# Sparse attention with a mixture block: the top-32 mask made on VectorE by a compare-and-multiply instead of signs on ScalarE and products on GpSimd

## The chip, the cores and the metric

The kernel runs on one core of a Trainium2 chip. Its engines work side by side, each through its own instructions in order: PE (TensorE, matmuls), DVE (VectorE), ACT (ScalarE), POOL (GpSimd) and SP, which issues the DMAs. The metric is the device time of one execution in microseconds; less is better.

## The reference

```python
scores = scale * np.matmul(q, k.transpose(0, 1, 3, 2))          # (4, 8, 576, 576), scale = 1/8
kth = np.partition(scores, -top_k, axis=-1)[..., -top_k:-top_k + 1]   # top_k = 32
mask = scores >= kth
scores = np.where(mask, scores, -1000000000.0)
scores = scores - np.max(scores, axis=-1, keepdims=True)
attn = np.exp(scores)
attn = attn / (np.sum(attn, axis=-1, keepdims=True) + 1e-09)
out = np.matmul(attn, v)
```

Its result goes, for each of the four batches, through two dense blocks (called MoE in the kernel): a rotation of x by angles x @ w_theta, mixing over tokens and channels, a ReLU residual, then a gated block with a normalisation and an output product. All of it is in float32.

## The kernel before

**Tiles.** Four batches of four visits (two heads each), nine tiles of 128 rows of scores to a visit: 144 tiles, worked in 72 pairs (G = 2). For each pair, DVE finds the 32 largest scores of every row.

**Attention of a pair, by lines.** PE makes scores into PSUM (L429), ACT copies them to `x` (L433; three buffers). `topk` on DVE: a network of maxima and minima that halves the candidates (L448, L449, first 576 wide, then 288), MAX8 on the losers (L452), then four rounds of MAX8 (L458) and three of MATCH_REPLACE (L461) on 160 candidates. `mx[:, :, 0]` is then the row maximum, `mx[:, :, 31]` the 32nd. A flag (L465) tells whether the network may have dropped a candidate; a second, exact pass at the end runs only if one is set. ACT makes two of the three columns of `cf` (L469, L470: minus an eighth of the maximum; a rounding margin), DVE the third (L471: the negated threshold). `weigh`, for each tile of the pair: ACT takes the sign of score minus threshold into `sg` (L480), then the exponential in place in `x` (L481); POOL multiplies both into `sg` (L482). `transpose`: PE turns `sg` (L491) and ACT clips it with ReLU into `ptb` (L492), so that negative products become zero. `values`: PE multiplies with v and a column of ones (L502, L513, L516); ACT takes the result (L522, L526), DVE and POOL divide (L542 to L547).

**Around it.** In the first pairs DVE, ACT and POOL also turn the 64-bit weights to float32 pairs (L147 to L194). From the second batch on, the MoE work of the batch before is woven in: matmuls into `ps_m` (L552 to L554, three for each product, from high and low parts), with helpers on DVE, ACT and POOL that all record L568. The last batch's MoE work follows when attention is over.

**Order.** The loop writes pair after pair: `topk` of pair g, `weigh`, `transpose` and `values` of pair g - 1, `scores` of a later pair, and a quota of MoE work between them. A scheduler with priorities then sets each engine's order: an instruction goes where it is expected to be ready. On the chip each engine keeps that order.

Of the kernel before, what the change touches and what calls it, by code (L numbers as in the profile page):

```python
# [10 lines left out]
F32 = mybir.dt.float32  # L11
F32R = mybir.dt.float32r
I32 = mybir.dt.int32
AF = mybir.ActivationFunctionType
OP = mybir.AluOpType
# [1 line left out]
NEG = -3.0e38  # L17
MAGIC = 12582912.0
TURN = 6.283185
ULP = 1.25 * 2.0 ** -24  # L20
LN_EPS = 1e-6


# [1 line left out]
def sparse_attention_then_moe_kernel(  # L25
# [21 lines left out]
    B, H, D, S = qT.shape  # L47
# [4 lines left out]
    G = 2  # L52
# [15 lines left out]
    att = ctx.enter_context(tc.tile_pool(name="att", bufs=2))  # L68
# [6 lines left out]
    act, dve, pool, pe = nc.scalar, nc.vector, nc.gpsimd, nc.tensor  # L75

    def f32(ap):
        return ap.bitcast(F32)
# [237 lines left out]
    def run(exact):  # L316
# [93 lines left out]
            nc.sync.dma_start(extra[p, 0:D], v[b, 2 * j + 1, r])  # L410

        GATE = {}
        X, SG, MX, PT = {}, {}, {}, {}
        PER = NP * NT

        def scores(n):
# [17 lines left out]

        def topk(g):

            x = X[g]
            mx = att.tile([128, G, 32], F32, name="mx")
            mm = att.tile([128, G, S], F32, name="mm", bufs=1)
            if exact:  # L440
                src, mr = ([t[:, i] for i in range(G)] for t in (x, mm))
            else:


                z = att.tile([128, G, QUARTER + 16], F32, name="z", bufs=1)
                for t, lo, mid, hi, win in ((x, 0, HALF, S, mm), (mm, 0, QUARTER, HALF, z)):
                    a, b = t[:, :, lo:mid], t[:, :, mid:hi]
                    dve.tensor_tensor(win[:, :, 0:mid], a, b, op=OP.max)  # L448
                    dve.tensor_tensor(mm[:, :, mid:hi], a, b, op=OP.min)  # L449
                for k, losers in enumerate((slice(LOSERS, S), slice(QUARTER, LOSERS))):  # L450
                    for i in range(G):
                        dve.max(out=z[:, i, QUARTER + 8 * k:QUARTER + 8 * k + 8], in_=mm[:, i, losers])  # L452
                src = [z[:, i] for i in range(G)]
                mr = [mm[:, i, 0:QUARTER + 16] for i in range(G)]
            for r in range(4):
                top = [mx[:, i, 8 * r:8 * r + 8] for i in range(G)]
                for i in range(G):
                    last = dve.max(out=top[i], in_=src[i])  # L458
                if r < 3:
                    for i in range(G):  # L460
                        dve.match_replace(out=mr[i], in_to_replace=top[i], in_values=src[i], imm_value=NEG)  # L461
                    src = mr
            kth = mx[:, :, 31]
            if not exact:
                dve.tensor_tensor(flags[:, g], z[:, :, QUARTER + 7::8], mx[:, :, 31:32].to_broadcast([128, G, 2]),  # L465
                                  op=OP.is_gt)

            cf = att.tile([128, G, 3], F32, name="cf", bufs=3)
            act.activation(cf[:, :, 0], mx[:, :, 0], AF.Copy, scale=-0.125)  # L469
            act.activation(cf[:, :, 1], kth, AF.Abs, scale=ULP)  # L470
            dve.scalar_tensor_tensor(cf[:, :, 2], cf[:, :, 1], 1e-37, kth, op0=OP.max, op1=OP.subtract)  # L471
            MX[g] = cf
            GATE[g] = last.ins

        def weigh(n):
            x, cf = X[n // G][:, n % G], MX[n // G][:, n % G]
            if n % G == 0:
                SG[n // G] = att.tile([128, G, S], F32, name="sg", bufs=2)
            sg = SG[n // G][:, n % G]
            act.activation(sg, x, AF.Sign, bias=cf[:, 2:3])  # L480
            act.activation(x, x, AF.Exp, bias=cf[:, 0:1], scale=0.125)  # L481
            pool.tensor_tensor(sg, x, sg, op=OP.mult)  # L482

        def transpose(n):
            x = SG[n // G].rearrange("p i n -> p (i n)")
            pt = psum.tile([128, 5, 128], F32, name="ps_t")
            ptb = att.tile([128, 5, 128], F32, name="ptb", bufs=2)
            k = (5, 4)[n % G]
            for c in range(k):
                lo = (c + 5 * (n % G)) * 128  # L490
                pe.transpose(pt[:, c, :], x[:, lo:lo + 128], ident)  # L491
            act.activation(ptb[:, 0:k], pt[:, 0:k], AF.Relu)  # L492
            PT[n] = ptb

        def values(n):
# [84 lines left out]
        class Lag:  # L580
# [5 lines left out]
            def step(self, f=None):  # L586
                if self.q:
                    self.q.pop(0)()
                if f is not None:
                    self.q.append(f)  # L590
# [46 lines left out]
        class Front:  # L637
# [37 lines left out]
            def keep(self, pt, h, l, x, engine):  # L675
                n = x.shape[-1]
                uact.activation(h, pt, AF.Copy)
                udve.tensor_copy(x, pt[:, :, 0:n])
                for q in range(128 // n):
                    q = slice(q * n, (q + 1) * n)  # L680
                    engine.tensor_tensor(l[:, :, q], x, f32(h[:, :, q]), op=OP.subtract)
# [244 lines left out]
        N = len(tiles)  # L926
# [7 lines left out]
        def advance(quota):  # L934

            nonlocal work, credit
            credit += quota
            while work is not None and credit > 0:
                c = next(work, None)
                if c is None:  # L940
                    work = None
                    break
                credit -= max(c, 250)
            if work is None:
                credit = min(credit, 0.0)
# [16 lines left out]
        def at(f, n):  # L962
            if 0 <= n < N:
                late = tiles[n][2] == NP - 1
                with tc.high_priority(offset=AHEAD + (EDGE if late else 0)):
                    f(n)
# [29 lines left out]
            next(conv, None)  # L996
        for g in range(N // G + 2):
            with tc.high_priority(offset=AHEAD):
                if g < N // G:
                    topk(g)  # L1000
                    with tc.issue_after(GATE[g]):
                        if g:
                            next(conv, None)
                        if g == SPLIT:
                            for _ in conv:
                                pass
            n0 = G * g
            for i in range(G):
                step(n0 + i)
                at(weigh, n0 - G + i)  # L1010
            q = FIRST_QUOTA if n0 < PER else QUOTA
            for i in range(G):
                at(scores, n0 + G + 1 + i)
                advance(q)
                at(transpose, n0 - G + i)
                advance(q)
                if i == G - 1:
                    at(values, n0 - G + i)
# [4 lines left out]
        advance(1e12)  # L1023

    run(False)
    flagged = nc.values_load(count[0:1, 0:1], min_val=0, max_val=128)
    with tc.If(flagged > 0):
        run(True)
# [42 lines left out]
```

## Time and profile before

| | us |
|---|---|
| three timed runs | 1000.35, 992.66, 991.75 (median 992.66) |
| the profiled execution | 986.55 |
| its span, first to last instruction | 984.8 |
| busy: PE | 854.1 (87%) |
| busy: DVE | 837.5 (85%) |
| busy: ACT | 626.2 (64%) |
| busy: POOL | 546.2 (55%) |

How to read it: the busy shares are means over stretches with different limits, so the table of stretches below says more than they do. A PE instruction's end is modelled. A DVE instruction's time runs from its start to its end, so time in which it stands still counts as busy.

### The profile page before, as it was taken

The numbers are of one execution on the slowest core, as the hardware profiler recorded it, in microseconds if no ns is written. First come the engines' busy times: TensorE is split into PE (matmuls) and PEld (weight loads), VectorE is DVE, ScalarE is ACT, GpSimd is POOL, SyncE is SP. The second block draws the span as 40 slices with busy tenths as digits, with TensorE's granted clock in tenths as the row PEclk, the third lists the DMA queues.
The fourth block names the chain that finished last, engine by engine and source line by source line (L and its number), as shares of the span: only waits on it lengthen the run. The fifth ranks groups of instructions, "written<-read, shape, count | busy, mean of one in ns | idle before, by whom it ended". The sixth has DMA issues, their size and how long they took to land.

```text
span 984.8 us, 17792 instructions
## 1 busy us (share of the span) xinstructions
PE 854.1 (87%) x5802; PEld 785.8 (80%) x5802; DVE 837.5 (85%) x2710; ACT 626.2 (64%) x1298; POOL 546.2 (55%) x476
## 2 busy tenths in 40 slices
PE   3656677785898999898998999799899999999997
PEld 2555666664797988897898998698889998889987
DVE  6999999899999998899999998999999951463552
ACT  5666767678767567777867777577957764350121
POOL 1686776658685854758385656375655553420030
PEclk9865676687899999999999999899999999999999
DMA  7797774647638463544461844352742645341221
GB/s 218 222 333 224 238 220 150 171 139 203 219 105 241 164 167 140 157 150 100 147 162 32 276 152 144 126 161 71 229 138 68 258 155 181 156 181 52 103 86 53
DMA packets 79393, 159.76 MB, mean 162 GB/s; under 512 B 36143, under 2 KB 40239, under 8 KB 71866
## 3 DMA queue, kind: packets, MB, share of 16 engines
q1 hardware_dynamic: 79290, 158.53, 51.0%
q8 instruction: 48, 0.79, 0.3%
q14 instruction: 55, 0.45, 0.1%
HBM read 108.63 MB, written 23.32 MB: 134 GB/s over the span
## 4 chain that ended last, share of the span: by engine, by line
DVE 46%; PE 32%; ACT 7%; DMA 7%; issue 4%; POOL 3%; SPq 1%; DVEq 0%; ACTq 0%; POOLq 0%
DVE mm L449 8%; PE ps_m L552 7%; DVE mx L458 7%; PE ps_m L553 7%; PE ps_m L554 7%; DVE mm L461 7%; DVE z L452 5%; DVE mm L448 4%; PE ps_v L513 4%; PE ps_s L429 2%; PE ps_t L491 2%; DVE F L568 2%; DMA q<-hi 2%; DVE z L448 2%; DVE cf L471 2%
## 5 line engine op out<-in xcount | busy, mean ns | idle before, releaser
L482 POOL TENSOR_TENSOR sg<-x,sg 128x576 f32<-128x576 f32 x144 | 213.0, 1495 | 150.9 <-ACT x L481 90.9
L513 PE MATMUL ps_v<-vc,ptb 128*128 128x65 f32 (+1 forms) x1280 | 176.6, 277 | 15.1 <-ACT ptb L492 15.1
L513 PEld LDWEIGHTS ps_v<-vc,ptb 128*128 128x128 f32 (+1 forms) x1280 | 167.4, 201 | 24.4 <-ACT ptb L492 18.5
L491 PE MATMUL ps_t<-ident,sg 128*128 128x128 f32 x648 | 132.0, 305 | 42.2 <-POOL sg L482 33.5
L480 ACT ACTIVATE sg<-x,cf 128x576 f32<-128x576 f32 x144 | 103.8, 769 | 56.0 <-DVE cf L471 53.2
L491 PEld LDWEIGHTS ps_t<-ident,sg 128*128 128x128 f32 x648 | 93.7, 166 | 53.9 <-POOL sg L482 39.0
L458 DVE MAX8 mx<-mm 128x8 f32<-128x160 f32 x432 | 118.9, 313 | 0.0
L433 ACT ACTIVATE x<-ps_s 128x576 f32<-128x576 f32 x144 | 92.4, 642 | 32.0 <-POOL sg L482 16.8
L429 PE MATMUL ps_s<-k,q 128*128 128x288 f32 x256 | 91.2, 367 | 24.1 <-ACT x L433 15.0
L552 PE MATMUL ps_m<-w_t,zah 128*128 128x288 f32 (+2 forms) x272 | 98.7, 363 | 11.3 <-DVE F L568 6.7
L481 ACT ACTIVATE x<-x,cf 128x576 f32<-128x576 f32 x144 | 108.0, 767 | 0.1
L492 ACT ACTIVATE ptb<-ps_t 128x640 f32<-128x640 f32 (+1 forms) x144 | 92.4, 642 | 13.2 <-PE ps_t L491 12.3
L554 PE MATMUL ps_m<-w_t,zal 128*128 128x288 f32 (+2 forms) x272 | 96.6, 355 | 0.6 <-DVE zal L568 0.4
L553 PE MATMUL ps_m<-w_t,zah 128*128 128x288 f32 (+2 forms) x272 | 96.5, 355 | 0.0
L452 DVE MAX8 z<-mm 128x8 f32<-128x312 f32 (+1 forms) x288 | 89.5, 372 | 1.9
L552 PE MATMUL ps_m<-w_t,zbh 128*128 128x288 f32 x288 | 85.9, 301 | 3.2 <-DVE F L568 1.9
L461 DVE MATCH_REPLACE8 mm<-mx,mm 128x160 f32<-128x160 f32 x288 | 87.0, 309 | 0.0
L553 PE MATMUL ps_m<-w_t,zbh 128*128 128x288 f32 x288 | 85.4, 300 | 0.6 <-DMA w_t<-d_spl 0.6
L554 PE MATMUL ps_m<-w_t,zbl 128*128 128x288 f32 x288 | 84.3, 299 | 1.0 <-POOL zbl L568 1.0
L552 PE MATMUL ps_m<-ph,w_t 128*128 128x288 f32 x256 | 76.8, 301 | 8.1 <-DMA w_t<-d_chh 4.3
L429 PEld LDWEIGHTS ps_s<-k,q 128*128 128x128 f32 x256 | 55.8, 218 | 33.1 <-ACT x L433 24.6
L449 DVE TENSOR_TENSOR mm<-x 128x576 f32<-128x576 f32 x72 | 82.2, 1141 | 0.0
(175 smaller groups left out, 2391.4 us busy)
## 6 DMA issues: line engine op xcount, KB each, us to landing
k<-hi SPq DMA_DIRECT2D x60, 144.0 KB, 2.6
kl<-raw SPq DMA_DIRECT2D x60, 144.0 KB, 3.1
vc<-in_v_dram SPq DMA_DIRECT2D x48, 128.0 KB, 2.8
w_t<-d_trh SPq DMA_DIRECT2D x4, 1152.0 KB, 5.2
w_t<-d_trl SPq DMA_DIRECT2D x4, 1152.0 KB
out_dram<-t SPq DMA_DIRECT2D x32, 144.0 KB, 2.2
raw<-in_q_dram SPq DMA_DIRECT2D x15, 288.0 KB, 3.0
q<-hi SPq DMA_DIRECT2D x30, 144.0 KB, 2.8
```

The source lines that it names most:

```text
L429: pe.matmul(o, q, k[:, m], start=a == 0, stop=a == len(terms) - 1)
L449: dve.tensor_tensor(mm[:, :, mid:hi], a, b, op=OP.min)
L452: dve.max(out=z[:, i, QUARTER + 8 * k:QUARTER + 8 * k + 8], in_=mm[:, i, losers])
L458: last = dve.max(out=top[i], in_=src[i])
L461: dve.match_replace(out=mr[i], in_to_replace=top[i], in_values=src[i], imm_value=NEG)
L481: act.activation(x, x, AF.Exp, bias=cf[:, 0:1], scale=0.125)
L482: pool.tensor_tensor(sg, x, sg, op=OP.mult)
L491: pe.transpose(pt[:, c, :], x[:, lo:lo + 128], ident)
L513: pe.matmul(o, pt[:, c, q], chunks[:, c, slot], start=alone and c == 0, stop=not alone and i == 1 and c == 3)
L552: pe.matmul(out, ah, bh, start=first, stop=False)
L553: pe.matmul(out, ah, bl, start=False, stop=False)
L554: pe.matmul(out, al, bh, start=False, stop=last)
```

## The change

The exponentials no longer wait for the whole top-k. After the first round of MAX8, which gives the row maximum, ACT makes `most` (minus an eighth of it) and takes the exponentials from `x` into a tile of their own, `e`, which has the place and the two buffers of `sg`. When the 32nd largest is known, DVE does the rest in one instruction per tile (`keep`): where `x` >= 32nd, `e` stays, elsewhere it becomes 0. The signs (72 x 2), the margin (Abs), the threshold on DVE and the products on POOL are gone. `topk` becomes a generator with a stop after the exponentials, so that `keep` of pair g - 1 is written between the first round and the rest of pair g.

```diff
-X, SG, MX, PT = {}, {}, {}, {}
+X, E, MX, PT = {}, {}, {}, {}
@@ topk, in the loop over the rounds
                 for i in range(G):
                     last = dve.max(out=top[i], in_=src[i])
+                if r == 0:
+                    most = att.tile([128, G], F32, name="most", bufs=3)
+                    e = att.tile([128, G, S], F32, name="e", tag="sg", bufs=2)
+                    act.activation(most, mx[:, :, 0], AF.Copy, scale=-0.125)
+                    for i in range(G):
+                        act.activation(e[:, i], x[:, i], AF.Exp, bias=most[:, i:i + 1], scale=0.125)
+                    E[g], MX[g] = e, mx
+                    yield
@@ end of topk
-            cf = att.tile([128, G, 3], F32, name="cf", bufs=3)
-            act.activation(cf[:, :, 0], mx[:, :, 0], AF.Copy, scale=-0.125)
-            act.activation(cf[:, :, 1], kth, AF.Abs, scale=ULP)
-            dve.scalar_tensor_tensor(cf[:, :, 2], cf[:, :, 1], 1e-37, kth, op0=OP.max, op1=OP.subtract)
-            MX[g] = cf
             GATE[g] = last.ins
-        def weigh(n):
-            x, cf = X[n // G][:, n % G], MX[n // G][:, n % G]
...
-            act.activation(sg, x, AF.Sign, bias=cf[:, 2:3])
-            act.activation(x, x, AF.Exp, bias=cf[:, 0:1], scale=0.125)
-            pool.tensor_tensor(sg, x, sg, op=OP.mult)
+        def keep(g):
+
+            x, e, mx = X.pop(g), E[g], MX.pop(g)
+            for i in range(G):
+                dve.scalar_tensor_tensor(e[:, i], x[:, i], mx[:, i, 31:32], e[:, i], op0=OP.is_ge, op1=OP.mult)
@@ transpose
-            act.activation(ptb[:, 0:k], pt[:, 0:k], AF.Relu)
+            act.activation(ptb[:, 0:k], pt[:, 0:k], AF.Copy)
@@ main loop
+                steps = topk(g) if g < N // G else iter(())
+                next(steps, None)
+                if 0 < g <= N // G:
+                    keep(g - 1)
+                next(steps, None)
                 if g < N // G:
-                    topk(g)
...
-                at(weigh, n0 - G + i)
```

What the scheduler makes of it on DVE, at the border of two pairs in the middle of the program (pair 49 begins with L448 on `x`). Before:

```order
L458 MAX mx<-mm 128x8 x2
L465 TENSOR_TENSOR flags<-z,mx 128x4
L448 TENSOR_TENSOR mm<-x 128x2x288
L449 TENSOR_TENSOR mm<-x 128x2x288
L471 SCALAR_TENSOR_TENSOR cf<-cf,mx 128x2
L448 TENSOR_TENSOR z<-mm 128x2x144
L449 TENSOR_TENSOR mm<-mm 128x2x144
L452 MAX z<-mm 128x8 x4
```

After, at the same place (L472 is the flag, L480 the new instruction):

```order
L458 MAX mx<-mm 128x8 x2
L480 SCALAR_TENSOR_TENSOR e<-x,mx,e 128x576
L472 TENSOR_TENSOR flags<-z,mx 128x4
L448 TENSOR_TENSOR mm<-x 128x2x288
L449 TENSOR_TENSOR mm<-x 128x2x288
L480 SCALAR_TENSOR_TENSOR e<-x,mx,e 128x576
L566 TENSOR_SCALAR st<-st 128x1
L448 TENSOR_TENSOR z<-mm 128x2x144
```

The two L480 of the ended pair stand around the first two instructions of the next pair, ahead of its first round, and the tiny L471 is gone. (L566 is the MoE helper, L568 before.)

On PE, around the last transposes of the last pair. Before, in the middle of the product of the gate (`zah`):

```order
L554 MATMUL ps_m<-zah,w_t 128x288
L491 MATMUL ps_t<-ident,sg 128x128 x3
L513 MATMUL ps_v<-vc_103,ptb 128x65 x3
L491 MATMUL ps_t<-ident,sg 128x128
L513 MATMUL ps_v<-vc_103,ptb 128x65
L516 MATMUL ps_v<-vm_104,ptb 128x65
L552 MATMUL ps_m<-zah,w_t 128x288
```

After, in the next stage of the same batch, the mixing over tokens (`zbh`, `zbl`):

```order
L489 MATMUL ps_t<-ident,e 128x128
L511 MATMUL ps_v<-vc_103,ptb 128x65
L489 MATMUL ps_t<-ident,e 128x128
L511 MATMUL ps_v<-vc_103,ptb 128x65
L514 MATMUL ps_v<-vm_104,ptb 128x65
L552 MATMUL ps_m<-w_t,zbl 128x288 x3
L892 MATMUL ps_m<-w_t,zbh 128x288
```

The last transposes stand later in the MoE work: behind them come 1062 matmuls into `ps_m` before, and 931 after.

On ACT in after, one of the 36 pairs where other instructions stand between `most` (L462) and the exponentials (L464):

```order
L566 ACTIVATE zbl<-one 64x512 [waits PE_49]
L462 ACTIVATE most<-mx 128x2 [waits DVE_49]
L432 ACTIVATE x<-ps_s 128x576 [waits PE_49]
L566 ACTIVATE ph<-F 128x288 [waits DVE_49]
L464 ACTIVATE e<-x,most 128x576 [waits Activation_49]
L464 ACTIVATE e<-x,most 128x576
L490 ACTIVATE ptb<-ps_t 128x512 [waits PE_49]
```

A copy of scores that waits for PE (L432) and a MoE copy that waits for DVE stand ahead of the two exponentials there.

## Rows read from the trace of the kernel before

**Rows 1.** Table of stretches: us; busy PE, PEld, DVE, ACT, POOL; clock; DMA

```profile
0.00:301.00 301.00, 213.27 (x1162) 184.03 (x1163) 287.60 (x895) 207.99 (x412) 199.50 (x185) 0.77 0.67 204
301.00:797.00 496.00, 462.78 (x3436) 436.06 (x3435) 475.83 (x1619) 359.81 (x765) 301.43 (x245) 0.98 0.49 152
797.00:814.00 17.00, 17.00 (x122) 15.92 (x121) 4.59 (x24) 11.49 (x26) 7.39 (x9) 1.00 0.46 174
814.00:985.00 171.00, 161.02 (x1089) 149.75 (x1088) 69.44 (x175) 46.94 (x98) 37.85 (x40) 0.99 0.32 117
```

**Rows 2.** Instructions of a line: ns min/median/max, first and last start us, forms

```profile
L448 DVE TENSOR_TENSOR mm<-x x72: 696/752/3183, 12.0 to 787.1; 128x576 f32<-128x576 f32 x72
L448 DVE TENSOR_TENSOR z<-mm x72: 440/447/1687, 13.4 to 789.9; 128x288 f32<-128x288 f32 x72
L449 DVE TENSOR_TENSOR mm<-x x72: 743/754/6581, 12.7 to 787.9; 128x576 f32<-128x576 f32 x72
L449 DVE TENSOR_TENSOR mm<-mm x72: 402/457/1577, 13.9 to 790.4; 128x288 f32<-128x288 f32 x72
L465 DVE TENSOR_TENSOR flags<-z,mx x72: 147/164/2337, 20.6 to 796.8; 128x4 uint8<-128x4 f32 x72
L471 DVE SCALAR_TENSOR_TENSOR cf<-cf,mx x72: 100/156/1522, 20.7 to 797.7; 128x2 f32<-128x2 f32 x72
```

**Rows 3.** Groups by line: busy us, mean ns | idle before, and its releasers

```profile
L448 DVE TENSOR_TENSOR mm<-x 128x576 f32<-128x576 f32 x72 | 69.0, 958 | 11.4 <-ACT x L433 11.1
L448 DVE TENSOR_TENSOR z<-mm 128x288 f32<-128x288 f32 x72 | 35.7, 495 | 0.0
L449 DVE TENSOR_TENSOR mm<-x 128x576 f32<-128x576 f32 x72 | 82.2, 1141 | 0.0
L449 DVE TENSOR_TENSOR mm<-mm 128x288 f32<-128x288 f32 x72 | 41.2, 572 | 1.3
L465 DVE TENSOR_TENSOR flags<-z,mx 128x4 uint8<-128x4 f32 x72 | 29.1, 404 | 1.3
L471 DVE SCALAR_TENSOR_TENSOR cf<-cf,mx 128x2 f32<-128x2 f32 x72 | 28.9, 402 | 1.0 <-ACT cf L470 0.6
L482 POOL TENSOR_TENSOR sg<-x,sg 128x576 f32<-128x576 f32 x144 | 213.0, 1495 | 150.9 <-ACT x L481 90.9 <-issue 40.2 <-ACT cf L469 13.8
```

**Rows 4.** Timeline of DVE and POOL from 499 us: start, us, instruction

```profile
499.38 2.17 DVE L448 TENSOR_TENSOR mm<-x 128x576 f32<-128x576 f32 x1
501.47 2.10 DVE L449 TENSOR_TENSOR mm<-x 128x576 f32<-128x576 f32 x1
503.50 1.52 DVE L471 SCALAR_TENSOR_TENSOR cf<-cf,mx 128x2 f32<-128x2 f32 x1
...
499.38 5.62 POOL L568 TENSOR_TENSOR zbl<-xn,zbh 128x640 fp32r<-128x640 f32 x3
```

**Rows 5.** Timeline of DVE from 772 us, a pair with a free POOL

```profile
772.73 0.54 DVE L458 MAX8 mx<-z 128x8 f32<-128x160 f32 x2
...
776.79 0.77 DVE L465 TENSOR_TENSOR flags<-z,mx 128x4 uint8<-128x4 f32 x1
777.48 0.75 DVE L448 TENSOR_TENSOR mm<-x 128x576 f32<-128x576 f32 x1
778.15 0.74 DVE L449 TENSOR_TENSOR mm<-x 128x576 f32<-128x576 f32 x1
778.82 0.15 DVE L471 SCALAR_TENSOR_TENSOR cf<-cf,mx 128x2 f32<-128x2 f32 x1
```

**Rows 6.** Groups by line and shape: scalar_tensor_tensor on DVE

```profile
L148 DVE SCALAR_TENSOR_TENSOR w_f<-w_raw,w_f 128x512 int32<-128x512 int32 x16 | 12.0, 752 | 0.0
L568 DVE SCALAR_TENSOR_TENSOR st<-st 128x2 f32<-128x2 f32 (+1 forms) x64 | 14.8, 232 | 1.7
```

**Rows 7.** Timeline of PE: the last transpose, and matmuls of the tail

```profile
813.99 0.28 PE L491 MATMUL ps_t<-ident,sg 128*128 128x128 f32 x1
838.70 0.56 PE L554 MATMUL ps_m<-w_t,zbl 128*128 128x288 f32 x3
```

## The prediction: what bounds the kernel, the change part by part, and the numbers

> **What bounds the kernel now.** I read the table of stretches first [rows 1]. The profiled execution falls into three parts. Up to 301 us VectorE (DVE) is busy 287.60 us of 301 and TensorE (PE) only 213.27: DVE sets the pace alone. From 301 to 797 us DVE is busy 475.83 of 496 and PE 462.78: DVE still has the least room, 20 us, with PE close behind at 33. The last flags row starts at 796.8 us [rows 2], so the last top-k ends there. After it PE is full: it is busy all of the next 17 us and 161.02 of the last 171. The time is therefore the end of the last top-k (T, now 797) plus a tail that PE works off (now 984.8 - 797 = 188 us).
>
> In the first two parts DVE is busy 287.60 + 475.83 = 763.4 us of 797, and 33.6 us idle. So whatever DVE gets on top must show, beyond those 33.6 us. But not all of its busy time is work. The two large maxima and minima at L448 and L449 have medians of 752 and 754 ns [rows 2] and means of 958 and 1141 ns [rows 3]. The timeline shows the reason: at 499.38 us an L448 takes 2.17 us while three GpSimd subtractions run for 5.62 us, the L449 behind it takes 2.10, and a two-element L471 takes 1.52 [rows 4]. With a free GpSimd the same lines take 0.75, 0.74 and 0.15 us [rows 5]. I read it so: a DVE instruction with two SBUF inputs stands still while GpSimd (POOL) works on SBUF data. The lost time, 72 times mean less median in each of six rows, is 14.8 (L448, 576 wide), 27.9 (L449, 576 wide), 3.5 and 8.3 (the 288-wide ones), 17.3 (L465) and 17.7 us (L471) [rows 2, 3]: 89.5 us, of which 71.8 without L471.
>
> **The change part by part.** *Added on DVE:* 144 scalar_tensor_tensor of 128x576 (L480 of after), two SBUF inputs each. No row of before has just this one. The nearest are the max and min of the same width: with GpSimd free, one starts 0.67 us behind the other (777.48 to 778.15 to 778.82) [rows 5]. A scalar_tensor_tensor costs no more per element than these: 128x512 with two inputs has a mean of 752 ns, standing still included [rows 6]. 144 x 0.67 = **+96.5 us**.
>
> *Removed on DVE:* 72 L471, busy 28.9 us in all [rows 3]: **-28.9**.
>
> *Removed on POOL:* 144 products, 213.0 us busy [rows 3], of the POOL's 199.50 + 301.43 + 7.39 + 37.85 = 546.2 [rows 1], so 39%. If they caused the standing still in proportion, their end would give back 0.39 x 71.8 = 28 us; if they always lay beside the MAX8 instructions, which do not stand still (L458, 0.54 us for two in rows 5), nothing. The product follows the exponential, which follows cf, so it mostly falls into the next pair's MAX8: I take half, **-14**.
>
> *New standing still:* the 144 new instructions have two SBUF inputs too. The five remaining kinds lose 71.8 us in 360 instructions, 0.20 us each; 61% of that stays when the products are gone: 144 x 0.12 = **+18**. Bounds: none, and as often as L449 loses today, 144 x 0.387 = 56 us. The Trainium skill, page "SBUF — State Buffer", section "Who interferes with whom", says that such an instruction contends with a GpSimd instruction that reads SBUF and that the later one waits until the earlier has finished; the 2.17 us of rows 4 agree. By that rule, with POOL still busy about 288 us of 876 and half of 1.5 us (the mean of the products in rows 3) to wait for, the estimate would be 144 x 0.33 x 0.75 = 36 us in place of 18, and the end 18 us later.
>
> *Moved:* the scheduler puts more MoE work ahead of the last transposes: 1062 matmuls into ps_m stand behind them on PE before, 931 after. On DVE this brings 2 F instructions and 36 small st ones ahead of the last top-k; at 232 ns for an st one [rows 6] and 0.45 for F, **+9 us**. The tail gets shorter: the trace of before has 931 such matmuls left in the row at 838.70 us [rows 7], that is 146 us before the end. Between the last top-k and the last transposes stand in after only the two new instructions (counted above) and a few matmuls; with those and the last values I take 6 us. Tail: **152 us in place of 188**. PE has the room: from 301 us to its last transposes (813.99) [rows 7] it is busy 462.78 + 17.00 = 480 us; 131 matmuls at 171/1062 = 0.16 us add 21, so 501 in a stretch that grows to some 550 (91%, now 93%).
>
> *Removed on ACT:* 144 Sign and 72 Abs. ACT is busy 359.81 of 496 [rows 1], so this frees time that nothing waits for: 0. *Moved on ACT:* the exponentials start after the first MAX8 pair (773.27) and are needed after the last one (776.79, the flags row) [rows 5]: 3.5 us for one small copy (about 0.2) and two exponentials (about 0.67 apart, as the 128x576 rows): 1.6 us. 2 us to spare: 0. If that cover is gone, DVE itself waits, with all its queue behind it. x is given back after the new product on DVE rather than after POOL's, which is no later: 0.
>
> Sum on DVE: 96.5 - 28.9 - 14 + 18 + 9 = +80.6 us, 1.1 us per pair. With the idle time unchanged T = 797 + 80.6 = 878 and the span is 878 + 152 = 1030 us; with the 1.8 us around the span, 1032. The profiled execution itself took 986.55 us, 6 below the median 992.66 of the three runs and 5 below the lowest; such offsets are as likely to go either way in the next runs, so I forecast **1030 us**.
>
> **The rivals.** *A, a free port: faster.* Place: L448, L449, L465. If without the products POOL's other work fits into the MAX8 stretches, all 71.8 us come back and the new instructions lose nothing: 96.5 - 28.9 - 71.8 + 9 = +5, T = 802, end 954; PE would just allow it (its 854 us of busy time plus the 87.7 us that it is idle in the first 301 make 942). It decides when the sum on DVE falls under +28 (T + 152 under 977 to 980, over 1% below the median with the 1.8 us). For it: the lost time is there. Against: POOL keeps 333 us of other work, and rows 4 show a subtraction, not a product, as the blocker. A middle case, a sum of +28 to +48, gives **no change**, about 990.
>
> *B, the old idle time takes it.* If DVE's waits of 33.6 us shrink to 14, because scores, PSUM results and weights come relatively earlier, 20 us go: 1010, still slower.
>
> *C, DVE waits for the exponentials.* In 36 of 72 pairs ACT's order has other instructions between `most` and the second exponential, many waiting on PE. If these 36 lose 0.6 us each: +22, 1052. Against: PE is less full than now.
>
> *D, standing still as L449 today:* +56 in place of +18, and nothing given back: 1030 + 52 = 1082.
>
> **How the numbers follow.** The forecast, 1010 to 1050 with B within it, has 0.72; C 0.08 (1050 to 1060); D and worse 0.06 (above 1060); no change, with the stretch up to 1003, 0.09; A 0.05. A difference of 1% (10 us around 992.66) is about what a measurement of this kernel can tell from none. Slower: 0.72 + 0.08 + 0.06 = 0.86. The range leaves out A, most of the no-change case and D, together just under 0.2: 1000 to 1060.
>
> **What would show it.** Right: 144 L480 with a median near 750 ns and a mean of 0.85 to 0.95; the last top-k at about 878 us and DVE busy above 95% up to there; the tail from there near 152 us; L448 and L449 with means a little lower than now; PE busy about 91% in the middle. Wrong: means of L448 and L449 near their medians (A); DVE idle before L480 on ACT (C); last top-k before 850 us; or PE still full when DVE ends, so that the tail stays near 188 us (then the end is 36 us later).

## The result, and the profile after

The changed kernel takes 1005.68 us (median of 1003.28 to 1006.95) where the kernel before takes 992.78: a ratio of 1.0117, 95% interval 1.0068 to 1.0166. It is slower by 1.2%, where 1030 us, 3.8%, was forecast. The profiled execution took 1006.95 us, its span 1005.1. The trace of the kernel before is of an execution 6 us under that kernel's median, so the two traces differ by 20.3 us where the medians differ by 12.9.

The table of stretches of the changed kernel, columns as in rows 1 (us; busy PE, PEld, DVE, ACT, POOL; clock; DMA share; GB/s), cut first at the end of the last MAX8 of the last pair, then by parts:

```profile
0.00:849.68 849.68, 723.70 (x4815) 661.43 (x4815) 803.30 (x2621) 492.59 (x1000) 295.97 (x296) 0.88 0.55 170
849.68:1005.07 155.39, 143.26 (x987) 134.70 (x987) 73.46 (x162) 41.18 (x83) 36.17 (x37) 0.99 0.28 101
...
0.00:327.00 327.00, 227.92 (x1233) 197.37 (x1234) 300.64 (x920) 186.17 (x360) 132.04 (x147) 0.75 0.65 198
327.00:851.00 524.00, 496.95 (x3593) 465.23 (x3592) 503.98 (x1704) 307.33 (x643) 165.25 (x151) 0.96 0.48 151
```

The same cut of the kernel before, at its last MAX8:

```profile
0.00:796.81 796.81, 675.86 (x4595) 619.89 (x4596) 763.27 (x2511) 567.65 (x1174) 500.74 (x430) 0.90 0.56 172
796.81:984.75 187.94, 178.21 (x1209) 165.86 (x1208) 74.19 (x199) 58.58 (x124) 45.43 (x47) 0.99 0.33 122
```

The shape of the forecast is there: the last top-k ends 52.9 us later, and the tail is 32.5 us shorter (155.4 us; 152 was forecast). What differs is the first number, 52.9 us in place of 81. Of it, 40.0 us are DVE's busy time (763.3 to 803.3) and 12.8 its idle time (33.5 to 46.4).

DVE's groups by line in the changed kernel (busy us, mean ns | idle before, and who ended it), to be held against [rows 3]:

```profile
L480 DVE SCALAR_TENSOR_TENSOR e<-x,mx,e 128x576 f32<-128x576 f32 x144 | 139.7, 971 | 5.9 <-ACT e L464 5.7
L449 DVE TENSOR_TENSOR mm<-x 128x576 f32<-128x576 f32 x72 | 60.7, 843 | 0.0
L448 DVE TENSOR_TENSOR mm<-x 128x576 f32<-128x576 f32 x72 | 58.2, 808 | 2.2 <-ACT x L432 2.2
L449 DVE TENSOR_TENSOR mm<-mm 128x288 f32<-128x288 f32 x72 | 37.2, 517 | 0.9
L448 DVE TENSOR_TENSOR z<-mm 128x288 f32<-128x288 f32 x72 | 35.7, 496 | 0.1
L472 DVE TENSOR_TENSOR flags<-z,mx 128x4 uint8<-128x4 f32 x72 | 24.2, 336 | 0.0
```

A single L480 takes longer than forecast (971 ns on average, where 0.85 to 0.95 us was the sign of being right), but L449 fell from 1141 to 843 ns and L448 from 958 to 808 [rows 3], with a median of 751 ns for both (754 and 752 before): they stand still far less. The timeline of DVE at a place where POOL does not interfere, to be held against [rows 5] (start, us, instruction):

```profile
177.93 0.81 DVE L480 SCALAR_TENSOR_TENSOR e<-x,mx,e 128x576 f32<-128x576 f32 x1
178.66 0.75 DVE L448 TENSOR_TENSOR mm<-x 128x576 f32<-128x576 f32 x1
179.33 0.75 DVE L449 TENSOR_TENSOR mm<-x 128x576 f32<-128x576 f32 x1
180.00 0.81 DVE L480 SCALAR_TENSOR_TENSOR e<-x,mx,e 128x576 f32<-128x576 f32 x1
180.73 0.15 DVE L472 TENSOR_TENSOR flags<-z,mx 128x4 uint8<-128x4 f32 x1
```

A free L480 takes 0.73 us from its start to the next, an L448 0.67 as taken.

### The profile page after: what moved, and what is told of

Same layout as the page of the kernel before. It is cut to its first block, busy times and chain, and to the rows that moved or that the text cites. A ratio compares the mean times of both kernels' runs of the same rounds, so it can differ in the third digit from the quotient of the medians.

```text
span 1005.1 us, 17503 instructions
## 1 busy us (share of the span) xinstructions
PE 867.0 (86%) x5802; PEld 796.1 (79%) x5802; DVE 876.8 (87%) x2782; ACT 533.8 (53%) x1082; POOL 332.1 (33%) x332
## 4 chain that ended last, share of the span: by engine, by line
PE 42%; DVE 28%; DMA 12%; ACT 6%; POOL 5%; SPq 3%; issue 3%; ACTq 0%; POOLq 0%; DVEq 0%
PE ps_m L550 9%; PE ps_m L552 9%; PE ps_m L551 9%; DVE e L480 6%; PE ps_v L511 6%; PE ps_s L428 4%; DVE mm L469 4%; DVE mx L458 3%; PE ps_t L489 3%; DVE mm L449 3%; DMA k<-hi 2%; DMA q<-hi 2%; DVE mm L448 2%; DMA raw<-in_q_dram 2%; DVE z L452 2%
## 5 line engine op out<-in xcount | busy, mean ns | idle before, releaser
L489 PE MATMUL ps_t<-ident,e 128*128 128x128 f32 x648 | 142.8, 313 | 66.9 <-DVE e L480 59.1
L511 PE MATMUL ps_v<-vc,ptb 128*128 128x65 f32 (+1 forms) x1280 | 181.9, 279 | 18.0 <-ACT ptb L490 17.8
L511 PEld LDWEIGHTS ps_v<-vc,ptb 128*128 128x128 f32 (+1 forms) x1280 | 172.7, 203 | 28.6 <-ACT ptb L490 21.5
L432 ACT ACTIVATE x<-ps_s 128x576 f32<-128x576 f32 x144 | 92.9, 645 | 146.0 <-DVE e L480 103.8
L489 PEld LDWEIGHTS ps_t<-ident,e 128*128 128x128 f32 x648 | 97.7, 170 | 82.7 <-DVE e L480 39.6
L480 DVE SCALAR_TENSOR_TENSOR e<-x,mx,e 128x576 f32<-128x576 f32 x144 | 139.7, 971 | 5.9 <-ACT e L464 5.7
L550 PE MATMUL ps_m<-w_t,zah 128*128 128x288 f32 (+2 forms) x272 | 99.5, 366 | 6.8 <-DVE F L566 4.7
L464 ACT ACTIVATE e<-x,most 128x576 f32<-128x576 f32 x144 | 103.8, 769 | 1.2
L551 PE MATMUL ps_m<-w_t,zah 128*128 128x288 f32 (+2 forms) x272 | 97.9, 360 | 0.0
L452 DVE MAX8 z<-mm 128x8 f32<-128x312 f32 (+1 forms) x288 | 90.0, 372 | 1.9
L566 POOL TENSOR_TENSOR pl<-F,ph 128x288 fp32r<-128x288 f32 x52 | 47.6, 923 | 116.7 <-ACT ph L566 97.0
L428 PE MATMUL ps_s<-kl,q 128*128 128x288 f32 x256 | 81.4, 329 | 1.3 <-DMA kl<-raw 1.3
L373 POOL TENSOR_TENSOR raw<-raw,hi 128x576 fp32r<-128x576 f32 x30 | 46.8, 1559 | 107.5 <-ACT hi L372 91.0
```

The costliest lines, as they stand in the source:

```text
L428: pe.matmul(o, q, k[:, m], start=a == 0, stop=a == len(terms) - 1)
L432: act.activation(x.rearrange("p (c n) -> p c n", c=2), ps[:, :, 0:HALF], AF.Copy)
L464: act.activation(e[:, i], x[:, i], AF.Exp, bias=most[:, i:i + 1], scale=0.125)
L480: dve.scalar_tensor_tensor(e[:, i], x[:, i], mx[:, i, 31:32], e[:, i], op0=OP.is_ge, op1=OP.mult)
L511: pe.matmul(o, pt[:, c, q], chunks[:, c, slot], start=alone and c == 0, stop=not alone and i == 1 and c == 3)
L550: pe.matmul(out, ah, bh, start=first, stop=False)
```

## The experiments

Ten kernels were run. Four were to tell whether the price of the removed products, or the place of the new instruction, was mis-sized; the later ones where that price comes from. This table holds the time, the ratio to the kernel before with its interval, the busy time of DVE and POOL over the whole span, and the end T of the last MAX8. Each ratio is taken to executions of the kernel before that were timed beside that kernel (their medians lie between 991.3 and 995.0 us), so it compares two rows better than their times do. DVE, POOL and T are those of one profiled execution.

| kernel | us | ratio (95%) | DVE | POOL | T |
|---|---|---|---|---|---|
| before | 992.8 | | 837.5 | 546.2 | 796.8 |
| after | 1005.7 | 1.0117 (1.0068 to 1.0166) | 876.8 | 332.1 | 849.7 |
| e1 before, no products | 957.1 | 0.9592 (0.9556 to 0.9628) | 776.9 | 324.0 | 755.8 |
| e2 after, products added | 1106.9 | 1.1110 (1.1069 to 1.1150) | 999.1 | 560.3 | 949.2 |
| e3 after, no masking | 961.7 | 0.9643 (0.9609 to 0.9677) | 773.0 | 324.9 | 738.3 |
| e4 after, half masking | 978.6 | 0.9800 (0.9753 to 0.9847) | 834.3 | 334.9 | 812.5 |
| e5 e1 with memsets | 952.3 | 0.9595 (0.9539 to 0.9650) | 789.3 | 487.1 | 766.0 |
| e6 before, L471 to ACT | 1006.8 | 1.0144 (1.0087 to 1.0201) | 839.5 | 555.4 | 821.6 |
| e7 after, second tile's masking on POOL | 1041.3 | 1.0494 (1.0439 to 1.0549) | 892.2 | 619.5 | 859.1 |
| e8 before, products held back | 989.0 | 0.9959 (0.9937 to 0.9980) | 828.1 | 550.3 | 800.2 |
| e9 e8 with L471 to ACT | 1001.6 | 1.0092 (1.0060 to 1.0124) | 837.6 | 546.5 | 799.9 |
| e10 e2, products held back | 1032.3 | 1.0405 (1.0350 to 1.0460) | 912.4 | 506.6 | 877.8 |

### e1: the kernel before without the products

```diff
-            act.activation(x, x, AF.Exp, bias=cf[:, 0:1], scale=0.125)
-            pool.tensor_tensor(sg, x, sg, op=OP.mult)
+            act.activation(sg, x, AF.Exp, bias=cf[:, 0:1], scale=0.125)
```

> The kernel before without GpSimd's 144 products: the exponential overwrites the sign in sg, so the mask is left out of the result. Theory P (the products hold the port that DVE's two-input instructions need, directly and by keeping GpSimd's other work queued up): the means of L448 and L449 at 576 wide fall to about 0.8 and 0.85 us as in the changed kernel, DVE loses 60 us or more of busy time in all, the last top-k ends at 735 to 755 us, and TensorE becomes the limit, time 935 to 960. Theory Q (the products hardly matter, the time given back in the changed kernel came from where the new instruction stands): means of L448 and L449 stay above 0.95 and 1.1 us, DVE loses 30 us or less, last top-k at 770 to 795, time 965 to 985.

DVE's busy time fell by 60.6 us, as theory P said, and T by 41 to 755.8. (L449 stayed at 914 ns, above the 0.85 us of theory P.) Its groups by line:

```profile
L449 DVE TENSOR_TENSOR mm<-x 128x576 f32<-128x576 f32 x72 | 65.8, 914 | 0.0
L448 DVE TENSOR_TENSOR mm<-x 128x576 f32<-128x576 f32 x72 | 58.5, 812 | 13.2 <-ACT x L433 12.8
L449 DVE TENSOR_TENSOR mm<-mm 128x288 f32<-128x288 f32 x72 | 35.6, 495 | 0.6
L471 DVE SCALAR_TENSOR_TENSOR cf<-cf,mx 128x2 f32<-128x2 f32 x72 | 24.7, 342 | 5.8 <-ACT cf L470 5.5
L465 DVE TENSOR_TENSOR flags<-z,mx 128x4 uint8<-128x4 f32 x72 | 21.9, 304 | 1.3
```

Nothing was done to these instructions, yet L449 went from 1141 to 914 ns and L448 from 958 to 812. The 576-wide pair, the narrow L449 and L465 gave back 39.6 us (72 times the differences of the means), L471 another 4.3; the remaining 17 us lie in other DVE instructions, weight conversion and MoE helpers. T moved by less than the busy time, since DVE then idles 56.1 us of 755.8 instead of 33.5.

### e3: the changed kernel without the masking

```diff
-            for i in range(G):
-                dve.scalar_tensor_tensor(e[:, i], x[:, i], mx[:, i, 31:32], e[:, i], op0=OP.is_ge, op1=OP.mult)
```

> The changed kernel without the 144 masking instructions on DVE (the mask is left out of the result). If DVE sets the end of the top-k: their 129 us of DVE time go, of which some 20 come back as standing still of L448, so the last top-k ends at 735 to 755 us; 1236 MoE matmuls stand behind the last transposes, so the tail is 195 to 210 us and the time 935 to 960, with TensorE now the limit. If the masking lies largely beside waits that DVE has anyway, the last top-k ends after 790 us and the time is above 975.

T came to 738.3 and the tail to 223 us, because 1236 MoE matmuls were left behind it; the time, 961.7, lies 1.7 us above what was expected. DVE lost 103.8 us, not the 139.7 that L480 was busy:

```profile
L449 DVE TENSOR_TENSOR mm<-x 128x576 f32<-128x576 f32 x72 | 68.9, 956 | 0.0
L448 DVE TENSOR_TENSOR mm<-x 128x576 f32<-128x576 f32 x72 | 63.5, 882 | 3.0 <-ACT x L432 2.2
```

L448 and L449 are slower again, 882 and 956 ns in place of 808 and 843. The first L480 of a pair stands ahead of them in the queue, so this fits waits that L480 takes on itself and that otherwise fall on them.

e1 and e3 cut the change into three steps in DVE's busy time, which add up because each starts where the one before ends: products away 837.5 to 776.9 (-60.6); signs and L471 away and the exponentials moved ahead 776.9 to 773.0 (-3.9); masking added 773.0 to 876.8 (+103.8). Sum: +39.3, as measured.

### e4: half of the masking

```diff
-                dve.scalar_tensor_tensor(e[:, i], x[:, i], mx[:, i, 31:32], e[:, i], op0=OP.is_ge, op1=OP.mult)
+                dve.scalar_tensor_tensor(e[:, i, 0:HALF], x[:, i, 0:HALF], mx[:, i, 31:32], e[:, i, 0:HALF],
+                                         op0=OP.is_ge, op1=OP.mult)
```

> The changed kernel with the masking on only the first 288 of 576 columns (the other half is left unmasked). If DVE sets the end of the top-k and an element costs the same throughout: 144 x 0.30 = 43 us less on DVE, last top-k at 805 to 815 us, 995 matmuls behind the last transposes, time 965 to 980. If standing still rather than elements makes the new instruction's cost: less than 25 us, time above 980.

DVE lost 42.5 us and T 37, the time 27, since the tail grew to 172 us. The loss is that of L480 itself, from 139.7 us in the changed kernel:

```profile
L480 DVE SCALAR_TENSOR_TENSOR e<-x,mx,e 128x288 f32<-128x288 f32 x144 | 97.1, 675 | 8.1 <-ACT e L464 6.4 <-PE ps_s L428 1.7
```

So the elements of L480 are paid for on the path at 0.30 us per 288, as forecast from L448.

### e2: products put back into the changed kernel

```diff
+                pool.tensor_tensor(x[:, i], e[:, i], e[:, i], op=OP.mult)
```

> The changed kernel with 144 GpSimd products of 128x576 put back (exponential times itself, written over the used-up scores, which nobody reads). Theory P: GpSimd is as full as before the change, DVE's standing still comes back with 45 to 60 us, the last masking ends at 895 to 910 us and the time is 1045 to 1065. Theory Q: DVE gets at most 20 us more, time 1005 to 1025.

The products add work on used-up data, which nobody reads. The direction was right and the size far off: DVE gained 122 us, 0.85 us per product, and the time is 1106.9, above even the 1065 of theory P. As many products of that size cost DVE 0.42 us each in the kernel before (60.6 / 144), though each takes longer there when nothing holds it up (median 1.43 us, against 1.15 in e10, where a product reads one tile twice). The groups by line show who ends POOL's wait:

```profile
L481 POOL TENSOR_TENSOR x<-e 128x576 f32<-128x576 f32 x144 | 227.4, 1581 | 208.8 <-DVE e L480 155.3 <-DVE flags L472 21.3 <-DVE st L567 18.8
L449 DVE TENSOR_TENSOR mm<-x 128x576 f32<-128x576 f32 x72 | 99.7, 1385 | 0.0
L449 DVE TENSOR_TENSOR mm<-mm 128x288 f32<-128x288 f32 x72 | 63.8, 886 | 1.0
L448 DVE TENSOR_TENSOR z<-mm 128x288 f32<-128x288 f32 x72 | 60.9, 846 | 0.1
```

Here a product is released by L480 itself, and so starts just where L449 and the two 288-wide instructions follow: 138 of the 144 products lie beside a DVE instruction with two SBUF inputs, and 35 do in the kernel before (counted over the rows of both engines, with more than 0.05 us side by side). That raised the question whether the place of a product sets its price, or its number.

### e10: the same products, held back

```diff
@@ topk, behind the MAX8 on the losers
+                Z[g] = z
@@ keep, behind the masking
+            z = Z.get(g + 1, x)
+            after = pool.tensor_scalar(turn, z[:, 0, QUARTER:QUARTER + 1], 1.0, 0.0, op0=OP.mult, op1=OP.add)
+            with tc.issue_after(after.ins):
+                for i in range(G):
+                    pool.tensor_tensor(x[:, i], e[:, i], e[:, i], op=OP.mult)
```

> The changed kernel with the 144 GpSimd products of e2 (on used-up data, read by nobody), but held back until the next pair's first MAX8 on the losers is done, by a tiny GpSimd instruction that reads its result. The number and size of the products are those of e2; only their start differs. If the price of a product is set by where it starts: DVE's busy time, 877 without products and 999 in e2, comes to 890 to 930, last masking at 865 to 905, time 1020 to 1060. If each product costs 0.85 us wherever it stands: DVE 990 or more, time 1095 to 1115. If the products then push the other GpSimd work into the two-input stretch as much as they leave it: DVE 930 to 990, time 1060 to 1095.

(The lines that make `turn` and `Z` are left out here.) In the trace 933 MoE matmuls lie behind the last transposes, as in that of the changed kernel. The products are those of e2; their start differs, and a tiny instruction (L485) is added that holds them back. DVE's busy time is 912.4: 35.6 us over the changed kernel, 0.25 us per product in place of 0.85, and the time 1032.3 in place of 1106.9.

```profile
L488 POOL TENSOR_TENSOR x<-e 128x576 f32<-128x576 f32 x144 | 163.9, 1158 | 0.7 <-DVE e L483 0.7
L451 DVE TENSOR_TENSOR mm<-x 128x576 f32<-128x576 f32 x72 | 66.2, 919 | 0.0
L451 DVE TENSOR_TENSOR mm<-mm 128x288 f32<-128x288 f32 x72 | 40.1, 557 | 1.1
L485 POOL TENSOR_SCALAR turn<-z 128x1 f32<-128x1 f32 x71 | 13.6, 192 | 137.8 <-DVE z L454 137.4
```

The narrow L451 (L449 of the changed kernel) is back from 886 to 557 ns. Both engines gain: the products, now beside MAX8, take 1158 ns instead of 1581; 22 of 144 still meet a two-input instruction. Between e2 and e10, then, the price of one and the same product is set by where it starts. That MAX8 does not stand still beside a product can be read in the trace of the kernel before: 317 of its MAX8 on 160 columns lie beside one and take 313 ns on average, 97 lie beside no POOL instruction and take 312.

### e5: GpSimd held without reading

```diff
-            pool.tensor_tensor(sg, x, sg, op=OP.mult)
+            pool.memset(x, 0.0)
+            pool.memset(x, 0.0)
```

(and the exponential into `sg`, as in e1; the mask is left out of the result.)

> As the kernel before without products (e1), but with two GpSimd memsets of 128x576 over the used-up scores where each product stood: GpSimd's queue is held about as long, without reading anything. Theory D (each GpSimd instruction that reads holds DVE up by itself): DVE's busy time stays as in e1, 772 to 785 us, and the means of L448 and L449 at 576 wide near 0.81 and 0.83 us. Theory K (what costs is the full queue, which pushes GpSimd's other work into DVE's two-input stretch): if the memsets fill GpSimd by 150 us or more, DVE's busy time rises to 795 to 810. In both the time stays below 985.

The memsets keep POOL busy:

```profile
L482 POOL MEMSET x<- 128x576 f32 x144 | 83.0, 580 | 148.2 <-ACT sg L481 147.8
L483 POOL MEMSET x<- 128x576 f32 x144 | 82.9, 581 | 4.3
L449 DVE TENSOR_TENSOR mm<-x 128x576 f32<-128x576 f32 x72 | 70.3, 976 | 0.0
L448 DVE TENSOR_TENSOR mm<-x 128x576 f32<-128x576 f32 x72 | 62.4, 866 | 12.0 <-ACT x L433 11.3
```

166 us of them, in place of 213 of products, raise DVE's busy time from 776.9 to 789.3, a fifth of what the products cost. The measurement lies between the two expectations (D up to 785, K from 795), about as near the one as the other. The memsets themselves hold no max or min up: eleven 576-wide L448 and L449 ran beside nothing but memsets on POOL, and took 748 to 759 ns, as free ones do. The Trainium skill, page "SBUF — State Buffer", section "Who interferes with whom", states that a DVE instruction with two SBUF inputs contends with a GpSimd instruction that reads SBUF and not with one that only writes it; these eleven agree. So what these two lines lost against e1 (8.4 us) came with the fuller queue, which moves POOL's other work.

This does not show that the rest of the 60.6 us is the products' own reading. In the kernel before, the products lie only 13 us beside the wide L448 and L449, which gave back 26.9 us in e1. Over all DVE instructions, the time beyond each one's free time comes to some 129 us in the kernel before and 70 in e1, nearly all of it beside some POOL instruction; at most 35 us lie beside a product (estimates from the rows of both engines; in e2 up to 119 do). The other 25 or so of the 60.6 must have come through POOL's other work, which runs at other times without the products. Why the memsets cost less by that way is not shown; they held POOL for a shorter time.

### e6 and e9: the threshold made by ScalarE

```diff
-            dve.scalar_tensor_tensor(cf[:, :, 2], cf[:, :, 1], 1e-37, kth, op0=OP.max, op1=OP.subtract)
+            for i in range(G):
+                act.activation(cf[:, i, 2:3], kth[:, i:i + 1], AF.Identity, bias=cf[:, i, 1:2], scale=-1.0)
```

> The kernel before with the threshold column made by two tiny ScalarE instructions per pair instead of the tiny DVE instruction L471 (28.9 us busy, 17.7 of it standing still). If DVE sets the end and the standing still goes with the instruction: DVE busy 837 to 812, last top-k near 772, time 970 to 980. If the standing still only passes to the next two-input instruction: DVE busy 822 to 828, last top-k near 785, time 980 to 990.

> As e8, and the threshold column made by ScalarE instead of L471 (as in e6). If in e6 it was the products' earlier start into DVE's two-input stretch that took the gain away: with them held back DVE loses 15 to 29 us more than e8, time 945 to 970. If it was ScalarE's longer chain: time no better than e8, or worse.

Neither gained anything. In e6 DVE's busy time is 839.5 with L471 gone, where 812 to 828 was expected, and it idles 56.8 us before T (16.0 of them for the copies of scores on ACT, now fuller); the time is 1006.8. With the products held back (e9), DVE has 837.6 us against 828.1 in e8. Its groups, and under them those of e8:

```profile
L450 DVE TENSOR_TENSOR mm<-x 128x576 f32<-128x576 f32 x72 | 80.9, 1124 | 15.5 <-ACT x L434 15.0
L451 DVE TENSOR_TENSOR mm<-x 128x576 f32<-128x576 f32 x72 | 79.5, 1104 | 0.0
```

```profile
L450 DVE TENSOR_TENSOR mm<-x 128x576 f32<-128x576 f32 x72 | 71.1, 988 | 13.2 <-ACT x L434 12.6
L451 DVE TENSOR_TENSOR mm<-x 128x576 f32<-128x576 f32 x72 | 73.3, 1018 | 0.0
L474 DVE SCALAR_TENSOR_TENSOR cf<-cf,mx 128x2 f32<-128x2 f32 x72 | 20.0, 278 | 1.3 <-ACT cf L473 1.1
```

The 20.0 us of the tiny instruction (L474 here) are gone, and L450 and L451 at 576 wide alone stand 9.8 and 6.2 us longer. This fits a wait that falls on whatever stands first in the two-input stretch: remove that, and its neighbour takes it. But it is not all: DVE's other instructions gained 29.5 us in e9, more than the 20.0 that left. The products also lay worse, beside two-input instructions for 50 us in e9 against 36 in e8 (and 79 in e6 against 46 in the kernel before). These two runs do not separate the two causes.

### e7: one tile of each pair masked on GpSimd

```diff
-            for i in range(G):
-                dve.scalar_tensor_tensor(e[:, i], x[:, i], mx[:, i, 31:32], e[:, i], op0=OP.is_ge, op1=OP.mult)
+            dve.scalar_tensor_tensor(e[:, 0], x[:, 0], mx[:, 0, 31:32], e[:, 0], op0=OP.is_ge, op1=OP.mult)
+            pool.tensor_scalar(x[:, 1], x[:, 1], mx[:, 1, 31:32], None, op0=OP.is_ge)
+            pool.tensor_tensor(e[:, 1], x[:, 1], e[:, 1], op=OP.mult)
```

> The changed kernel with the masking of the second tile of each pair on GpSimd (a compare, then a product; 144 GpSimd instructions). DVE loses 72 x 0.89 = 64 us. If GpSimd instructions placed there cost DVE 0.42 us each as the products did in the kernel before: 60 us come back and the time is 1000 to 1012. If they cost 0.85 us each as in e2: 1030 to 1060. If only the products cost, and the compare nothing: about 975 to 1000.

1041.3 us, DVE 892.2: half of the masking less on DVE, and yet 15 us more than in the changed kernel. The groups of the two GpSimd instructions:

```profile
L480 POOL TENSOR_SCALAR x<-x,mx 128x576 f32<-128x576 f32 x72 | 187.1, 2598 | 124.0 <-DVE mx L458 26.3 <-ACT e L464 24.6 <-PE ps_t L490 14.1
L481 POOL TENSOR_TENSOR e<-x,e 128x576 f32<-128x576 f32 x72 | 109.3, 1518 | 3.8
```

The compare falls in the two-input stretch like e2's products: all 72 lie beside a two-input instruction, and 55 of the 72 products do. With a mean of 2598 ns, where the shortest takes 1719, it also stands still itself. The masking on DVE fell by 65.8 us (139.7 to 73.9), so the 144 GpSimd instructions cost DVE about 81 us, 0.56 us each; how much of it is the compare and how much the product is not separated.

### e8: the products of the kernel before, held back

```diff
@@ in place of the product in weigh
+            after = pool.tensor_scalar(turn, z[:, 0, QUARTER:QUARTER + 1] if z is not None else x[:, 0, 0:1], 1.0, 0.0,
+                                       op0=OP.mult, op1=OP.add)
+            with tc.issue_after(after.ins):
+                for i in range(G):
+                    pool.tensor_tensor(sg[:, i], x[:, i], sg[:, i], op=OP.mult)
```

(Other lines are left out: `weigh` without its product stands ahead of `topk` in the loop, and `topk` stops after L452 for this.)

> The kernel before with its 144 products held back until the next pair's first MAX8 on the losers (L452) is done: a tiny GpSimd instruction reads that result first, and the products of the pair are queued behind it, so that they start in DVE's stretch of MAX8 and MATCH_REPLACE, which reads one SBUF input. If the price of a product is set by where it starts: DVE's busy time 785 to 805, last top-k at 760 to 780, time 955 to 975. If each product costs DVE 0.42 us wherever it stands: DVE 837 as before, time 985 to 1000. If holding GpSimd back pushes its other work into the two-input stretch: DVE above 837, time above 1000.

DVE fell only by 9.4 us, T rose by 3 in the profiled execution, and the time is 989.0: 0.4% under the kernel before (interval 0.2 to 0.6), the fastest kernel here that does the whole computation. The gain expected (a time of 955 to 975) was too large because it took the products of the kernel before for badly placed: 35 of them met a two-input instruction, and in e8 35 still do, with 36 us beside such instructions in place of 46. Against e1 the products held back cost DVE 51.2 us, 0.36 us each: holding back did not bring the 0.25 of e10 here, and these products are also the longer ones.

## Why the prediction was right and wrong

**Right: what sets the end.** T is set by DVE and the tail by what PE has left: 931 matmuls were to give 152 us, and the tail was 155.4. e3 and e4 move T by the DVE time taken out (103.8 us of it move T by 111, 42.5 by 37), and lengthen the tail by what is then left over. So the sign followed from the sum on DVE.

**Wrong: the step "removed on POOL", -14 us.** It took POOL's standing-still price as a share of POOL's busy time (39% of 71.8 us in five lines, 28) and then halved it, because the products would mostly lie beside MAX8. Measured by e1 it is -60.6 us of DVE time: 39.2 on the five lines of the sum, 4.3 on L471, 17 in weight and MoE instructions that the sum did not look at at all. The place was read rightly: 109 of the 144 products meet no two-input instruction, and MAX8 does not stand still (rows 5, with a free POOL, could not show that; e10's section does). The inference from the place to the price failed. The products also moved POOL's other work, and that stood in DVE's way: at most 35 of the 60.6 us lie beside a product (estimated under e5). Even the bound of 28 was no bound, since busy time is no measure of the price: e2 and e10 hold the same 144 products at 0.85 and 0.25 us each. This one step is off by 46.6 us, more than the whole miss.

**Wrong the other way: the step "removed on DVE", -28.9 us.** Of it 17.7 us were standing still, by the prediction's own rows. e1 to e3 shows -3.9 for L471 together with the signs and the earlier exponentials; in e6 and e9, without L471, DVE's busy time does not fall either. That its wait passes to the next two-input instruction fits both, and is not shown alone. Off by 25 us.

**Nearly right: the masking.** 96.5 + 18 = 114.5 us was forecast, e3 measures 103.8. Its parts were off: the bare instruction is 0.73 us, not 0.67 (+9; rows 6 did not bear out that it costs no more per element, since 752 ns for 512 columns is more than L448's 752 for 576), its mean of 971 ns holds 23 us of standing still over the free 0.81 (18 forecast; the other estimate, 36, was too much), and about 14 us were taken from L448 and the lines behind it. With the other two: 46.6 + 10.7 - 25.0 = 32.3 us less than the sum of 71.6 without the moved work, and that is the 39.3 measured.

**Not foreseen: idle time.** DVE idled 12.8 us more before T. That is a balance: the waits for late exponentials (rival C) add 5.7 us (the L480 row), the wait of L540 for ACT's copy of the attention result grew from 3.0 to 8.9 us and waits in the MoE work grew too, while the wait of L448 for the copies of scores fell from 11.1 to 2.2. The moved MoE work, +9, measures 6.6: DVE's MoE instructions behind T take 75.9 us in the kernel before and 69.3 in the changed one. In return 4.6 us of the last pair's masking fell behind T.

**The rivals.** A, the free port, had the right mechanism, in part: the prediction named L448 and L449 near their medians as its sign, and they came to 808 and 843 over 751. It got 5% because rows 4 show a subtraction as the blocker; a single case was read as the rule. Its price was nearer than the forecast's: all 71.8 us, where 60.6 were measured. That is partly luck, since only 39.2 of the 60.6 lie on the lines that the 71.8 counts. A had the masking in its sum at 96.5 us; what kept it from making the kernel faster is mainly the 25.0 us that L471 did not give back, then 11.2 us less from the products, 12.8 us of idle time, and 7.3 us that the masking cost more. B did not come (idle time rose), nor D; C came, but small: 5.7 us. PE was busy 497 of 524 us in the middle, 95% where 91% was forecast.

What stays open: why e5, with 12 us more on DVE than e1, is not slower than it (ratios 0.9595 and 0.9592). By the traces its T is 10 us later and its tail 16 us shorter, since about 1010 MoE matmuls lie behind the last transposes in place of 1119; why PE had got further by then, no run shows. How the 60.6 us split between the products' own reading and the work they moved is known only by the estimate under e5.

## What to carry to other kernels

Price a GpSimd instruction by where it starts against the other engine's two-input instructions, not by its busy time: find the means and medians of *all* the lines that stand still, and for the removal take the whole excess as one end of the range. An instruction that only waits in front of others can give little back when it is removed (L471: 24.7 us busy in e1, 3.9 less on DVE in e3, which has it no more), and can take over waits when it is added, so standing still is to be summed over a stretch and not per instruction. If such a product must stay, look how many meet that stretch, and hold them back if many do: it took the time from 1106.9 to 1032.3 us in e10, where 138 of 144 had met it, but only 0.4% off in e8, where 35 had.

## What the runs showed of the hardware

Not expected: one and the same 128x576 product on GpSimd cost 0.85 us of VectorE time as placed in e2 and 0.25 held back in e10, and its own mean fell from 1581 to 1158 ns. Memsets that held GpSimd for 166 us cost VectorE 12 us, where 213 us of products cost 60.6. And products that mostly met no two-input instruction still cost VectorE time through the work behind them in GpSimd's queue: at most 35 of the 60.6 us lie beside a product.
